# Late columns and block sums as single steps of one written-out order, and a second ScalarE function in the memory units

## The chip, the cores and the metric

The kernel runs on one core of one Trainium2 chip. The engines are TensorE (PE, matmuls), VectorE (DVE), ScalarE (ACT), GpSimd (POOL) and SyncE (SP), which issues the DMAs. Each engine works through its own queue in order. The metric is the device time of one execution in microseconds (us), as the median of several runs.

## The reference

All values are float32. B, H, S, D are 4, 8, 576, 64; there are 2304 tokens; the weights are 512x1536, 512x1536 and 1536x512.

```
scores = where(causal, -1e9, q @ k.T / sqrt(D));  a = softmax(scores)
local = a @ v
q_p = phi(q)                        # phi(x) = max(x, 0) + min(exp(x), 1)
mem_out = (q_p @ M_prev) / (q_p @ z_prev + 1e-6)
x = g * mem_out + (1 - g) * local   # g = sigmoid(beta), per head; heads side by side: 2304 x 512
out = ((x @ w_a) * (x @ w_b)) @ w_out
```

## The kernel before, in words

**Precision.** Each float32 operand of a matmul is split in two parts, a high one (an ACT copy in a shorter format) and a low one (DVE or POOL subtracts the high one). A product is three matmuls: high by high, high by low, low by high.

**Stages.** Attention first, for 16 pairs of heads (`schedule()`): `HEAD` lists the steps of the start by hand, `LOOP` the steps of one pair with lags, for pairs 3 to 8 and, in a second order, 9 to 13, and `TAIL` the steps of the end of attention and of what overlaps it. A step is `name.index`. A step's name stands for instructions on one engine or on two; every engine gets its instructions in the order of the list, and waits for others by semaphores. `BANKS` names the PSUM bank of each step that takes one.

Then come 48 *columns*: column `c` is one block of 384 tokens `t` and one of 12 slices `f` of the weights. `uA.c` and `uB.c` are its two hidden products (12 matmuls each), `ucx` copies B to SBUF (ACT), `umx` multiplies A into it (DVE), `uhh` and `uhl` split the result (ACT, DVE), and `uo.c` adds its output product to three accumulators (9 matmuls). After the last `f` of a `t`, `ua`, `ub`, `uc` bring the accumulators out. The columns cover t = 0 to 3.

The tokens of t = 4 and 5 are handled after them by `step7`, once per `f`: a scheme that multiplies block matrices with fewer products (in the manner of Strassen and Winograd). It needs sums of token blocks (`combine` makes T1, TT2, T3, T4 from the raw blocks B11, B12, B21, B22, which lie in one tile `xf`; `split_x` splits each into `xc`) and sums of weight blocks: `sums_load(f)` fetches the weights of `f` back from HBM into a ring inside `xf`, `sums_of(f)` forms the sums on POOL, `sums_split(f)` splits them (ACT, DVE). Rings 0 and 1 use the same place in `xf`, so the load of 1 waits for the split of 0.

x itself is made by memory *units*: one unit is one of four 128-wide parts `j` of x for one `t`. Its steps are those of `UNIT`: `load` (q by SP, two buffers), `phi`, `phi2`, `norm` to `norm3` (the division), `turn` (a transpose on DVE), `turn_h`, `turn_l` (split), `x_load` and `sums` (the attention part, added on POOL), `retrieve` (3 or 6 matmuls with M_prev), `join`, `join_h`, `join_l`. In `TAIL` a unit's step is `q_<step>.n` with t = 2 + n // 4 and j = n % 4.

**Order around the change.** `TAIL` reaches up to column 29 in its columns and up to unit 5 (and some steps of unit 6). From column `CUT` = 30 on, `column(c, between)` runs a fixed order: A, the planned unit steps of the first half, B, the four conversion steps, `done(c - 1)`; then the unit steps of the second half, then `arrange(c)`, which holds block sums, splits, pool changes and ring loads by column number. `TURN` gives the half columns of the units. In `step7` of f = 0, `sums_split(1)` and the loads of rings 2 and 3 stand ahead of the last token product and of `h1`.

**Before, `phi`** is an exponential on ACT (L1095) and a minimum with 1 on DVE (L1099), then `max(q, 0) + ph` (L1102).

Of the kernel before, what the change touches and what calls it, by code (L numbers as in the profile page):

```python
# [75 lines left out]
Kclamp.5 Khi.4 Kshift.5 Klo.4 uB.3 uhh.2 Kmag.6 uo.1 Khigh.5 Kclamp.6 Kload.7 uhl.2 Kload.10 Klow.5
ucx.3 Khi.5 Kload.9 Kshift.6 umx.3 uA.4 Klo.5 Kload.11 Kmag.7 uB.4 Khigh.6 Kclamp.7 Kload.12 uo.2
uhh.3 uA.5 Klow.6 uhl.3 Khi.6 ucx.4 Kshift.7 Khigh.7 Kmag.8 Kload.14 Klo.6 umx.4 uB.5 Kclamp.8 uhh.4
Klow.7 Kshift.8 Kload.13 uo.3 Khi.7 uA.6 uB.6 uhl.4 Kmag.9 Kclamp.9 ucx.5 Khigh.8 Klo.7 Klow.8
Kload.16 Khi.8 umx.5 uhh.5 uo.4 Kshift.9 Klo.8 uhl.5 Kmag.10 ucx.6 Kload.15 Khigh.9 Klow.9 Khi.9  # L80
Kmag.11 Kclamp.10 Kshift.10 uA.7 umx.6 Khigh.10 Kclamp.11 uB.7 Klo.9 uhh.6 Kload.18 Klow.10
Kshift.11 uhl.6 uo.6 Khi.10 Klo.10 Khigh.11 uA.8 ucx.7 Kmag.12 Klow.11 Khi.11 Kclamp.12 umx.7
Kload.17 Klo.11 Kload.20 uhh.7 uB.8 uo.5 Kshift.12 uhl.7 uA.9 Kmag.13 Khigh.12 Klow.12 uB.9 ucx.8
umx.8 uo.7 uhh.8 Kclamp.13 Khi.12 Kshift.13 Kload.19 Klo.12 Kmag.14 Khigh.13 ucx.9 uhl.8 Kclamp.14
uA.10 Klow.13 Khi.13 Klo.13 Kshift.14 umx.9 Kmag.15 uB.10 uhh.9 uhl.9 Khigh.14 ucx.10 Klow.14
Kclamp.15 uo.9 umx.10 Kshift.15 Khi.14 Klo.14 Kmag.16 Khigh.15 Klow.15 uhh.10 uA.11 Khi.15 uB.11
Kclamp.16 Kmag.17 ucx.11 uo.8 uA.12 Klo.15 uB.12 Kshift.16 uhl.10 Khigh.16 umx.11 Klow.16 Kclamp.17
uhh.11 Kshift.17 uo.10 Khi.16 uA.13 Khigh.17 Kload.22 Klo.16 Kmag.18 Klow.17 ucx.12 uhl.11 Kclamp.18
umx.12 Kshift.18 uhh.12 uB.13 Khi.17 uhl.12 uo.11 Kmag.19 uA.14 Klo.17 uB.14 Khigh.18 Klow.18 Khi.18
Klo.18 Kload.21 ucx.13 Kmag.20 uo.12 Kclamp.19 Kclamp.20 umx.13 uhh.13 Kshift.19 Kshift.20 ucx.14  # L90
Khigh.20 uhl.13 Klow.20 Khi.20 Khigh.19 uA.15 umx.14 Kmag.22 Kclamp.22 Klo.20 uhh.14 Klow.19
Kload.23 uhl.14 Kshift.22 uB.15 Khi.19 ucx.15 uo.13 Klo.19 umx.15 Kmag.21 uhh.15 Khigh.22 Kclamp.21
Klow.22 Khi.22 uA.16 Kshift.21 Khigh.21 uB.16 Klow.21 Khi.21 Kmag.23 uhl.15 Klo.21 uo.14 ucx.16
Kclamp.23 Klo.22 umx.16 Kshift.23 Khigh.23 Klow.23 uo.15 uA.17 Khi.23 Klo.23 uhh.16 uB.17 wo.0
uhl.16 q_load.0 uo.16 q_load.1 q_phi.0 ucx.17 q_phi2.0 q_norm.0 umx.17 Ms.0 q_norm2.0 q_norm3.0
uhh.17 uA.18 q_turn.0 Ml.1 uB.18 Mp.1 uhl.17 q_x_load.0 uo.17 ucx.18 umx.18 q_turn_h.0 ua.17 q_phi.1
q_turn_l.0 q_phi2.1 uhh.18 uA.19 ub.17 q_load.2 uhl.18 q_retrieve.0 q_norm.1 uB.20 q_norm2.1
q_norm3.1 uc.17 q_turn.1 q_sums.0 q_join.0 q_phi.2 uB.19 uA.20 uB.21 Wf.0 Wf.1 ucx.19 q_turn_h.1
umx.19 uhh.19 q_turn_l.1 uhl.19 Wf.2 uo.18 q_x_load.1 q_phi2.2 uo.19 q_norm.2 Ml.2 q_norm2.2
# [1521 lines left out]
```

## Time and profile before

| | |
|---|---|
| median of 3 runs | 669.57 us (669.0 to 669.58) |
| the profiled execution's own time | 671.89 us |
| its span, first to last instruction | 670.1 us |
| PE busy in it | 651.3 us, 97% |
| DVE, ACT, POOL busy | 516.4, 332.4, 277.2 us |
| mean granted clock of TensorE | 0.992 |

A share of busy time is an average over stages with different limits: in the pair loop four engines are busy nearly all of the time, in the columns PE alone. PE's gaps are few and can be read one by one in its timeline, each with the instruction that ended it. [...]

### The profile page before, as it was taken

How to read it: one execution, taken by the hardware profiler on the slowest of the kernel's cores; microseconds unless marked ns; L12 is line 12 of the kernel's file. 1: busy time of each engine (PE TensorE's matmuls, PEld its weight loads, DVE VectorE, ACT ScalarE, POOL GpSimd, SP SyncE). 2: the span in 40 equal slices, each digit the busy share in tenths (PEclk: the TensorE clock that was granted, in tenths of full speed). 3: DMA queues.
4: the chain of work that ended last, by engine and by line, in shares of the span. 5: the costliest groups of instructions: out<-in, count | busy, mean ns of one | idle time of the engine just before them, and what ended most of it. 6: DMA issues, size and time to landing. Idle time of an engine off the chain costs nothing.

```text
span 670.1 us, 11702 instructions
## 1 busy us (share of the span) xinstructions
PE 651.3 (97%) x4074; PEld 598.7 (89%) x4074; DVE 516.4 (77%) x1030; ACT 332.4 (50%) x794; POOL 277.2 (41%) x402
## 2 busy tenths in 40 slices
...
GB/s 180 198 189 133 150 138 187 119 193 188 266 75 134 210 153 110 187 127 59 150 109 206 120 122 30 56 112 66 48 48 31 142 31 65 64 32 63 1 32 63
DMA packets 130250, 76.85 MB, mean 115 GB/s; under 512 B 98704, under 2 KB 117392, under 8 KB 130192
## 3 DMA queue, kind: packets, MB, share of 16 engines
...
q8 instruction: 32, 0.52, 0.3%
q14 instruction: 26, 0.21, 0.1%
HBM read 55.64 MB, written 20.45 MB: 114 GB/s over the span
## 4 chain that ended last, share of the span: by engine, by line
PE 72%; DVE 17%; DMA 3%; ACT 2%; issue 2%; SPq 2%; POOL 1%; DVEq 0%; ACTq 0%; POOLq 0%
PE pp L921 24%; PE pp L1299 12%; PE o L959 12%; PE pt L196 5%; PE pw L710 4%; DVE PT L200 4%; PE pt L544 4%; PE o L1375 4%; DVE nm L583 3%; PE pr L1406 3%; PE m L1375 1%; PE pw L544 1%; DMA qr<-in_q_dram 1%; PE m L1164 1%; DVE wl L200 1%
## 5 line engine op out<-in xcount | busy, mean ns | idle before, releaser
L921 PE MATMUL pp<-xh,wh 128*128 128x384 f32 x376 | 126.9, 337 | 0.9 <-ACT x L934 0.9
L921 PE MATMUL pp<-xh,wl 128*128 128x384 f32 x376 | 126.5, 337 | 0.3 <-DVE wl L200 0.3
L921 PE MATMUL pp<-xl,wh 128*128 128x384 f32 x376 | 126.3, 336 | 0.0
L610 POOL TENSOR_SCALAR P<-P,sum 128x384 f32<-128x384 f32 (+4 forms) x144 | 80.8, 581 | 5.1 <-DVE sum L602 4.5
L1265 POOL TENSOR_TENSOR xf<-xf 128x256 f32<-128x256 f32 x48 | 38.6, 804 | 96.7 <-DMA xf<-ws 63.6
L921 PEld LDWEIGHTS pp<-xh,wh 128*128 128x128 f32 x376 | 70.9, 189 | 3.4 <-ACT x L934 1.9
L921 PEld LDWEIGHTS pp<-xl,wh 128*128 128x128 f32 x376 | 70.9, 189 | 1.6
L921 PEld LDWEIGHTS pp<-xh,wl 128*128 128x128 f32 x376 | 70.8, 188 | 0.6 <-DVE wl L200 0.6
L200 DVE TENSOR_TENSOR PT<-pt,PT 128x512 fp32r<-128x512 f32 (+2 forms) x112 | 62.7, 588 | 10.4 <-ACT PT L665 8.1
L593 ACT ACTIVATE P<-pt,nm 128x128 f32<-128x128 f32 (+3 forms) x128 | 66.9, 530 | 4.9 <-DVE nm L583 3.1
L710 PE MATMUL pw<-PT,vh 128*128 128x320 f32 (+4 forms) x416 | 63.0, 294 | 1.0 <-DVE PT L200 0.6
L710 PEld LDWEIGHTS pw<-PT,vh 128*128 128x128 f32 x416 | 57.6, 189 | 3.6 <-DVE PT L200 1.9
L959 PE MATMUL o<-wh,hh 128*128 128x512 f32 x144 | 57.2, 397 | 3.3 <-ACT hh L941 3.3
L583 DVE TENSOR_REDUCE nm<-pt 128x1 f32<-128x128 f32 (+3 forms) x128 | 55.9, 478 | 3.6 <-PE pt L544 3.3
L959 PE MATMUL o<-wh,hl 128*128 128x512 f32 x144 | 57.7, 400 | 0.0
L959 PE MATMUL o<-wl,hh 128*128 128x512 f32 x144 | 57.0, 396 | 0.0
L865 POOL TENSOR_SCALAR wt<-wt 128x512 f32<-128x512 f32 (+1 forms) x21 | 21.6, 1028 | 83.3 <-ACT wt L859 83.3
L196 PE MATMUL pt<-ident,P 128*128 128x128 f32 (+1 forms) x400 | 52.8, 276 | 2.3 <-POOL P L610 1.0
L665 ACT ACTIVATE PT<-pt 128x512 fp32r<-128x512 f32 (+2 forms) x112 | 52.6, 525 | 2.9 <-PE pw L710 1.7
L941 ACT ACTIVATE hh<-x 128x384 fp32r<-128x384 f32 x48 | 25.0, 522 | 55.4 <-DVE x L937 45.9
L934 ACT ACTIVATE x<-pp 128x384 f32<-128x384 f32 x47 | 22.8, 486 | 53.5 <-PE pp L921 37.5
L196 PEld LDWEIGHTS pt<-ident,P 128*128 128x128 f32 (+1 forms) x400 | 44.1, 140 | 5.8 <-POOL P L610 2.5
...
## 6 DMA issues: line engine op xcount, KB each, us to landing
...
```

The lines of the kernel that those rows point to most:

```text
L196: nc.tensor.transpose(out, x, ident[0:x.shape[0], 0:x.shape[0]])
L200: eng.tensor_tensor(out=lo, in0=x, in1=hi, op=ALU.subtract)
L544: nc.tensor.matmul(o, lhsT=w, rhs=x, start=first, stop=True, skip_group_check=True)
L583: nc.vector.tensor_reduce(out=s["nm"][:, c:c + 1], in_=src, axis=AX.X, op=ALU.min)
L593: nc.scalar.activation(out=s["P", i][:, h, :], in_=src, func=AF.Exp, scale=-1.0, bias=s["nm"][:, c:c + 1], accum_out=s["sums"][:, c, 0:1],)
L610: nc.gpsimd.tensor_scalar(out=pr[:, h, :], in0=pr[:, h, :], scalar1=r[:, c:c + 1], scalar2=1.0, op0=ALU.mult, op1=ALU.mult,)
L665: nc.scalar.activation(out=dst, in_=src, func=AF.Copy)
L710: nc.tensor.matmul(pv[:, a:hi], lhsT=w, rhs=x, start=(n == 0), stop=(n == len(ops) - 1))
L921: nc.tensor.matmul(pp, lhsT=w[:, w0:w0 + P], rhs=x[:, kk, :], start=(c == 0), stop=(c == 3 * KK - 1),)
L959: nc.tensor.matmul(po[t, m], lhsT=hx[:, m * P:(m + 1) * P], rhs=w[:, w0:w0 + DM], start=(f == ORDER[t][0] and n == 0), stop=(f == ORDER[t] ...
L1265: nc.gpsimd.tensor_tensor(out=o, in0=x, in1=y, op=op)
L1299: nc.tensor.matmul(o, lhsT=a[:, kk * P:(kk + 1) * P], rhs=b[:, kk, :], start=first and c == 0, stop=True, skip_group_check=True,)
```

## The change

- `HEAD`, `BANKS` and both orders of `LOOP` are other orders of the same steps, and so is the part of `TAIL` that was there.
- `TAIL` goes on to `uhl.47`: all 48 columns, all units and the block sums are single steps. `co`, `sh`, `sl` are combine, high split and low split of the n-th of B11, T1, TT2, T3, B21, T4, B22; `rl`, `ru`, `rs` are load, sums and split of a ring; `pi`, `cl`, `go` set up tiles and pools. `column`, `arrange`, `TURN` and the plan go. T4 and B22 are still split in `step7`.
- In units of t over 2, `phi` is relu(-q) and then exp(-that) on ACT, and the minimum on DVE goes.
- In `step7` of f = 0, `sums_split(1)` and `sums_load(3)` come behind `hl(0, h1)`, and the last output rows of column 47 behind these.
- The second "ob" pool has one buffer, and units of t over 3 use a new pool.

```diff
 HEAD = """
-id.0 zi.0 wm.14 mk.0 ib.0 Dk.0 zq.1 Dq.0 TK.0 TQ.0 zq.0 Dk.1 b_2.0 thK.0 Dq.1 Eq.0 tlK.0 TK.1 thQ.0
+zq.0 id.0 zi.0 ib.0 wm.14 Dk.0 Dq.0 mk.0 Dk.1 TK.0 Dq.1 TQ.0 thK.0 tlK.0 b_2.0 Eq.0 TK.1 b_3.0 thQ.0
...
 TAIL = """
...
-mag0.15 h2B.14 px.14 G0.15 n2.15 G5.15 clamp0.15 l2B.14 mag1.15 G3A.15 V1B.14 Kload.6 V2B.14 xA.14
-G2A.15 h0.15 shift0.15 G2B.15 h5.15 high0.15 n1.15 h2A.15 low0.15 hi0.15 h3A.15 G4.15 w_0.15 G1.15
...
-py.13 high2.15 V1B.15 V2B.15 xA.15 cx.15 low2.15 hi1.15 st_.14 mx.15 xB.15 lo1.15 hh.15 Kmag.3
-st_.15 Kclamp.3 pp.0 Khi.2 Kshift.3 uA.1 Kload.8 Klo.2 Khigh.3 uB.1 uA.2 ucx.1 hl.15 Klow.3 Kmag.4
...
+n4.15 V2A.14 l2B.14 V1B.14 n2.15 n1.15 mag1.15 shift0.15 high0.15 V2B.14 xA.14 low0.15 G5.15 G2A.15
+st_.12 h2A.15 G2B.15 px.14 clamp1.15 G3A.15 h5.15 G0.15 G4.15 hi0.15 h0.15 G1.15 G3B.15 l2A.15
...
+py.13 high2.15 V2B.15 low1.15 mx.15 st_.14 xA.15 xB.15 hh.15 hl.15 st_.15 low2.15 pp.0 hi1.15 lo1.15
+uA.1 Khi.2 Kload.7 Kmag.3 Kload.6 uB.1 Klo.2 Kclamp.3 ucx.1 Kshift.3 Khigh.3 uA.2 Kload.8 Kmag.4
...
+q_join.7 Ws.22 Ws.23 umx.33 uA.34 uo.31 q_join_h.7 q_join_l.7 uA.35 go.0 uhh.33 q_load.8 q_phi.8
+q_phi2.8 uB.34 q_norm.8 uhl.33 ucx.34 q_x_load.8 q_norm2.8 q_load.9 uo.32 umx.34 uhh.34 q_norm3.8
+q_turn.8 uB.35 q_phi.9 q_turn_h.8 uo.33 ucx.35 uB.36 q_x_load.9 uhl.34 uA.36 uB.37 q_sums.8 q_phi2.9
+umx.35 q_load.12 q_x_load.12 uA.37 q_load.13 uhh.35 q_sums.9 q_norm.9 q_turn_l.8 q_retrieve.8 uhl.35
+q_norm2.9 q_norm3.9 q_turn.9 q_sums.12 ucx.36 q_phi.12 umx.36 q_join.8 uo.34 q_turn_h.9 uhh.36 uo.35
+ucx.37 q_phi.13 pi.0 q_phi2.12 q_norm.12 q_turn_l.9 q_norm2.12 q_norm3.12 uc.35 uhl.36 q_x_load.13
+q_retrieve.9 q_turn.12 umx.37 q_join.9 q_turn_h.12 q_phi2.13 ua.35 uA.38 uhh.37 q_load.14 uA.39
+q_x_load.14 uB.38 uo.36 q_norm.13 sh.0 ucx.38 uhl.37 q_turn_l.12 uo.37 ub.35 q_norm2.13 uB.39 umx.38
+uhh.38 q_phi.14 ucx.39 q_norm3.13 q_retrieve.12 q_turn.13 uA.40 uhl.38 q_turn_h.13 umx.39 uB.40
+uhh.39 q_sums.13 q_phi2.14 q_load.15 q_x_load.15 uo.38 q_turn_l.13 uB.41 q_sums.14 q_load.10
+q_x_load.10 q_join.12 q_norm.14 ucx.40 q_retrieve.13 uhl.39 uo.39 q_norm2.14 umx.40 uhh.40 sl.0
+uA.41 q_norm3.14 q_turn.14 q_join.13 uB.42 uhl.40 q_turn_h.14 co.1 q_phi.15 q_sums.15 ucx.41
+q_turn_l.14 q_phi2.15 q_retrieve.14 uB.43 q_norm.15 q_norm2.15 umx.41 uo.40 q_norm3.15 uA.42 uhh.41
+q_turn.15 ucx.42 q_join.14 q_turn_h.15 uhl.41 q_phi.10 q_phi2.10 q_turn_l.15 umx.42 sh.1 uhh.42
+q_norm.10 ucx.43 uhl.42 q_retrieve.15 q_norm2.10 q_norm3.10 q_load.11 q_x_load.11 uA.43 umx.43
+q_sums.10 uo.41 q_phi.11 q_turn.10 q_join.15 q_phi2.11 uB.44 uo.42 uA.44 uhh.43 q_norm.11
+q_turn_h.10 uhl.43 q_norm2.11 q_norm3.11 sl.1 q_turn_l.10 ucx.44 uB.45 q_sums.11 q_retrieve.10
+q_turn.11 umx.44 co.3 q_join.10 q_turn_h.11 uo.43 uhh.44 q_turn_l.11 q_retrieve.11 uA.45 uB.46 sh.3
+co.2 uB.47 q_join.11 cl.0 uA.46 sh.2 sl.2 uhl.44 sh.4 ucx.45 umx.45 sl.3 sl.4 co.5 uo.44 rl.0 ru.0
+uA.47 uhh.45 ucx.46 uhl.45 umx.46 uhh.46 uhl.46 ucx.47 uo.45 umx.47 uo.46 rs.0 uhh.47 rl.1 ru.1
+uhl.47
 """
...
         def phi():
             ph = r["ph"] = pool.tile([P, J, U, Q4], F32, tag="ph", name="ph")
-            nc.scalar.activation(out=ph, in_=r["q"], func=AF.Exp)
+            if late:
+                nc.scalar.activation(out=ph, in_=r["q"], func=AF.Relu, scale=-1.0)
+                nc.scalar.activation(out=ph, in_=ph, func=AF.Exp, scale=-1.0)
+            else:
+                nc.scalar.activation(out=ph, in_=r["q"], func=AF.Exp)
 
         def phi2():
             ph = r["ph"]
-            nc.vector.tensor_scalar(
-                out=ph, in0=ph, scalar1=1.0, scalar2=None, op0=ALU.min
-            )
+            if not late:
+                nc.vector.tensor_scalar(
+                    out=ph, in0=ph, scalar1=1.0, scalar2=None, op0=ALU.min
+                )
...
-        sums_split(f + 1)
-        if f == 0:
+        if f:
+            sums_split(f + 1)
+            sums_load(f + 3)
+        else:
             sums_load(2)
-        sums_load(f + 3)
         prev[3]()
...
         hh(0, h1)
-        prev[4]()
-        hl(0, h1)
+        if f == 0:
+            hl(0, h1)
+            sums_split(1)
+            sums_load(3)
+            prev[4]()
+        else:
+            prev[4]()
+            hl(0, h1)
...
         attention(late, early, tiles, {"TK": first_weights, "S_4": turn_over}, more, beyond)
-        for c in range(CUT, len(columns)):
-            column(c, lambda: memory(c, True))
-            memory(c, False)
-            arrange(c)
```

## Rows read from the trace of the kernel before

**Rows 1.** The page's first part: the span, and PE's busy time.

```profile
span 670.1 us, 11702 instructions
PE 651.3 (97%) x4074; PEld 598.7 (89%) x4074; DVE 516.4 (77%) x1030; ACT 332.4 (50%) x794; POOL 277.2 (41%) x402
```

**Rows 2.** Windows: length, busy us (and instructions) of each engine, clock, DMA.

```profile
0.00:20.00 20.00, 17.20 (x128) 13.55 (x129) 14.56 (x36) 13.35 (x38) 11.47 (x24) 1.00 0.83 180
20.00:40.00 20.00, 18.74 (x162) 16.33 (x162) 19.21 (x44) 19.76 (x59) 17.87 (x30) 1.00 0.84 189
...
480.00:500.00 20.00, 17.39 (x82) 14.72 (x82) 16.37 (x39) 4.81 (x10) 2.53 (x2) 0.92 0.21 50
...
520.00:540.00 20.00, 16.57 (x76) 15.58 (x76) 11.27 (x18) 6.63 (x13) 9.42 (x12) 0.83 0.37 119
```

**Rows 3.** PE's timeline in the late columns: start, duration, instruction, idle before.

```profile
464.91 0.50 PE L959 MATMUL o<-wh,hh 128*128 128x512 f32 x1 [1.01 <-ACT hh L941]
...
480.64 0.45 PE L1164 MATMUL m<-yh,md 128*128 128x384 f32 x1 [0.19 <-ACT yh L1148]
...
481.69 0.34 PE L921 MATMUL pp<-xh,wh 128*128 128x384 f32 x1
...
495.40 0.50 PE L959 MATMUL o<-wh,hh 128*128 128x512 f32 x1 [2.25 <-ACT hh L941]
```

**Rows 4.** PE's timeline after the first step 7; 18 matmuls start from 532.22 on.

```profile
532.22 0.69 PE L1299 MATMUL pp<-xh,wh 128*128 128x384 f32 x1 [3.42 <-DVE h L1339]
...
538.04 0.34 PE L1299 MATMUL pp<-xeh,wh 128*128 128x384 f32 x1
```

**Rows 5.** The chain that ended last, 494 to 540: start, us, what.

```profile
496.16 2.72 PE o L959 x7
498.88 4.90 PE pp L921 x24
503.78 2.10 PE o L959 x9
...
506.54 4.20 PE pp L921 x24
...
520.82 3.19 DMA xf<-ws
```

**Rows 6.** Windows over the late columns and over four pairs of the loop.

```profile
432.00:518.00 86.00, 82.38 (x428) 75.04 (x427) 62.20 (x143) 21.99 (x44) 11.09 (x11) 0.98 0.24 60
30.20:76.80 46.60, 45.95 (x402) 41.18 (x402) 45.94 (x106) 45.38 (x129) 44.73 (x69) 1.00 0.67 168
```

**Rows 7.** Groups by line, 330 to 530: busy us, mean ns, idle before.

```profile
L1099 DVE TENSOR_SCALAR ph<-ph 128x384 f32<-128x384 f32 x14 | 6.6, 470 | 1.5 <-ACT ph L1095 1.5
...
L1095 ACT ACTIVATE ph<-q 128x384 f32<-128x384 f32 x13 | 6.7, 513 | 10.6 <-DVE q L1144 9.0 <-DMA z<-in_z_prev_dram 1.5
```

**Rows 8.** The program's only table load: ns, first and last start.

```profile
L520 ACT ACT_TABLE_LOAD  x1: 1283/1283/1283, 0.7 to 0.7; - x1
```

**Rows 9.** POOL's timeline at the sums of ring 0.

```profile
513.63 3.18 POOL L1265 TENSOR_TENSOR xf<-xf 128x256 f32<-128x256 f32 x4 [17.94 <-DMA xf<-ws]
```

**Rows 10.** DVE's timeline in the first step 7.

```profile
519.46 1.29 DVE L200 TENSOR_TENSOR wl<-xf,wh 128x768 fp32r<-128x768 f32 x2 [0.18 <-ACT wh L1278]
...
528.24 1.41 DVE L200 TENSOR_TENSOR sl<-xf,sh 128x768 fp32r<-128x768 f32 x1 [2.46 <-ACT sh L1278]
...
531.61 0.56 DVE L1339 TENSOR_TENSOR h<-pp,h 128x384 f32<-128x384 f32 x1
```

**Rows 11.** Timelines of POOL, PE and ACT where attention turns into columns.

```profile
192.56 0.94 POOL L353 TENSOR_SCALAR xh<-xx 128x384 fp32r<-128x384 f32 x1
...
196.61 1.86 PE L196 MATMUL pt<-ident,P 128*128 128x128 f32 x15 [0.98 <-POOL P L610]
...
210.55 0.49 ACT L934 ACTIVATE x<-pp 128x384 f32<-128x384 f32 x1 [0.76 <-POOL hl L200]
211.09 0.45 PE L921 MATMUL pp<-xh,wh 128*128 128x384 f32 x1 [0.86 <-ACT x L934]
```

More of the change, by code (lines that the diff above doesn't have):

```diff
@@ L76 @@
[L76 to L99, printed above, removed]
@@ L112 @@
[L112 to L114 removed]
+h3A.11 TK.14 b_3.13 l3A.11 S_3.13 pd.12 e4.12 r_.12 px.10 n3.12 pe.11 thK.14 pb.12 m3B.13 pf.11
+pc.12 TQ.14 V1A.11 V2A.11 tlK.14 n1.12 m3A.13 e3B.13 thQ.14 fw.0 b_.13 b_2.13 S_2.13 n4.12 xA.11
+m2A.13 Lp.13 m2B.13 e3A.13 e2A.13 S_.13 V1B.11 n0.12 e2B.13 mA.13 py.10 G5.12 V2B.11 eA.13 mB.13
@@ new lines @@
+Kshift.9 Khigh.9 Khi.8 Klo.8 uhl.5 Klow.9 Kmag.10 Khi.9 ucx.6 Klo.9 umx.6 Kload.12 Kmag.11 Kclamp.10
+Kload.15 Kshift.10 uA.7 Khigh.10 Klow.10 uB.7 uhh.6 uo.5 uA.8 uhl.6 Khi.10 Kclamp.11 Kshift.11
+Khigh.11 Klo.10 Klow.11 Kload.14 uB.8 ucx.7 Kmag.12 umx.7 uhh.7 uhl.7 uo.6 Khi.11 Klo.11 Kmag.13
+ucx.8 Kclamp.12 Kshift.12 Khigh.12 Klow.12 umx.8 uA.9 uB.9 uo.7 Kclamp.13 Kshift.13 Khigh.13
+Kload.17 uhh.8 Khi.12 uhl.8 Kmag.14 Klo.12 Klow.13 ucx.9 uA.10 umx.9 Khi.13 Kmag.15 uB.10 uhh.9
+Klo.13 uhl.9 Kload.16 uo.8 ucx.10 uA.11 Kclamp.14 Kshift.14 Khigh.14 Klow.14 Kclamp.15 Khi.14 umx.10
@@ new lines @@
+Kshift.15 uhh.10 Khigh.15 Kmag.16 Kclamp.16 Klo.14 Klow.15 uhl.10 uB.11 Khi.15 uo.9 Kshift.16 ucx.11
+Kmag.17 Klo.15 Kclamp.17 Khigh.16 umx.11 Kload.18 Klow.16 Khi.16 uhh.11 Kshift.17 Kmag.18 Khigh.17
+Kload.19 Klo.16 uA.12 uB.12 ucx.12 uo.10 uhl.11 Klow.17 umx.12 Khi.17 uhh.12 Kmag.19 uA.13 Kclamp.18
+uB.13 Kshift.18 Kclamp.19 Khigh.18 Klo.17 Klow.18 Khi.18 uo.11 uA.14 Kload.21 uhl.12 Kload.20 ucx.13
+uB.14 Kmag.20 Kshift.19 Klo.18 umx.13 uhh.13 Khigh.19 Klow.19 uhl.13 Kclamp.20 Kshift.20 Kload.22
@@ new lines @@
+Khigh.20 Klow.20 ucx.14 uo.12 Khi.19 umx.14 Klo.19 uA.15 Khi.20 Kmag.21 uhh.14 Kclamp.21 Kmag.22
+Klo.20 uhl.14 Kshift.21 uB.15 uo.13 ucx.15 Khigh.21 Kclamp.22 Klow.21 uA.16 Khi.21 Kshift.22
+Khigh.22 umx.15 uhh.15 uB.16 Klo.21 Klow.22 Kload.23 Kmag.23 uhl.15 Kclamp.23 Khi.22 ucx.16 Klo.22
+uo.14 uA.17 umx.16 uB.17 Kshift.23 Khigh.23 Klow.23 Khi.23 Klo.23 uhh.16 uo.15 wo.0 uhl.16 q_load.0
+q_phi.0 ucx.17 umx.17 q_x_load.0 uhh.17 q_phi2.0 q_norm.0 uA.18 uB.18 ucx.18 q_load.1 q_norm2.0
+uo.16 q_norm3.0 q_turn.0 uhl.17 q_sums.0 q_x_load.1 uo.17 umx.18 q_turn_h.0 q_phi.1 Ml.1 q_turn_l.0
@@ new lines @@
+uA.19 uhh.18 ua.17 q_phi2.1 q_norm.1 ub.17 uB.19 uc.17 Ms.0 q_norm2.1 Wf.0 Mp.1 q_retrieve.0
+q_norm3.1 q_load.2 Ws.0 Wf.1 uhl.18 Wf.2 q_join.0 q_turn.1 Wf.3 uB.20 Ws.3 q_turn_h.1 q_phi.2 ucx.19
+umx.19 q_phi2.2 q_join_h.0 q_norm.2 Ml.2 q_sums.1 uhh.19 Ws.2 q_turn_l.1 uhl.19 q_norm2.2 ucx.20
+q_join_l.0 uA.20 umx.20 uB.21 Wf.4 q_norm3.2 Wf.5 uhh.20 uo.18 Ws.1 uo.19 q_load.3 q_retrieve.1
+q_phi.3 Wf.6 q_join.1 uA.21 q_turn.2 uhl.20 q_phi2.3 q_turn_h.2 q_turn_l.2 q_x_load.2 Ws.5 Wf.7
+q_join_h.1 ucx.21 q_norm.3 uA.22 uB.23 umx.21 uB.22 q_sums.2 q_norm2.3 uhh.21 ucx.22 q_join_l.1
@@ new lines @@
+q_norm3.3 uo.20 Wf.8 uhl.21 umx.22 Ws.4 uhh.22 q_turn.3 Wf.9 Ws.7 uhl.22 q_retrieve.2 q_join.2
+q_turn_h.3 q_join_h.2 q_load.4 Ws.8 Wf.10 ucx.23 Ws.6 uo.21 Ws.9 uA.23 q_x_load.3 q_turn_l.3 umx.23
+uo.22 q_join_l.2 q_phi.4 uhh.23 q_phi2.4 q_sums.3 q_retrieve.3 q_load.5 uhl.23 uo.23 Wf.11 q_join.3
+q_join_h.3 q_join_l.3 uA.24 uB.24 q_norm.4 Ws.10 ua.23 ub.23 uc.23 ucx.24 q_norm2.4 umx.24 uhh.24
+p2.0 uB.25 uhl.24 ucx.25 uA.25 umx.25 uB.26 Wf.12 uA.26 q_norm3.4 uo.24 q_turn.4 Ws.11 uhh.25 Wf.13
+uA.27 uhl.25 Ws.13 q_turn_h.4 Wf.14 Wf.15 ucx.26 umx.26 q_phi.5 q_phi2.5 uB.27 q_x_load.5 q_norm.5
@@ new lines @@
+q_load.6 q_norm2.5 uB.28 q_turn_l.4 Mp.2 q_norm3.5 Ws.12 Ws.15 q_turn.5 uo.25 uhh.26 uhl.26 ucx.27
+umx.27 uB.29 q_phi.6 q_retrieve.4 q_phi2.6 uA.28 uhh.27 ucx.28 uhl.27 q_turn_h.5 uB.30 uo.26
+q_norm.6 q_norm2.6 uA.29 umx.28 uhh.28 uA.30 Ml.3 Wf.16 q_x_load.4 q_turn_l.5 uhl.28 Wf.17 ucx.29
+q_sums.4 q_norm3.6 q_join.4 q_load.7 umx.29 Ws.14 Wf.18 q_turn.6 Wf.19 q_turn_h.6 q_sums.5
+q_join_h.4 Ws.17 q_retrieve.5 q_turn_l.6 uo.27 Mp.3 uhh.29 uB.31 q_phi.7 Ws.16 q_phi2.7 uo.28 uhl.29
+Ws.18 Wf.20 q_join.5 q_norm.7 uA.31 q_norm2.7 uB.32 ucx.30 q_join_h.5 q_join_l.4 umx.30 q_norm3.7
```

194 lines of the change are left out of this document (74 added, 120 removed).

## The prediction, made before the change was run

> **What bounds the kernel now.** I read the page first: TensorE (PE) is busy for 651.3 of a span of 670.1 us [rows 1]. The order of a list cannot make a matmul shorter, so what an order can win is the rest, about 19 us, and whatever the clock loses. The table of windows says where that is: the first 40 us (17.20 and 18.74 busy of 20), then 480 to 500 (17.39, granted clock 0.92) and 520 to 540 (16.57, clock 0.83) [rows 2]. So I went to PE's timeline at those places and looked at what is named behind each "idle before".
>
> Three waits lie in the late columns. At 464.91 PE idles 1.01 for `hh`. At 480.64 it idles 0.19 for `yh`, and the three matmuls of a retrieve then take 1.05 (480.64 to 481.69). At 495.40 it idles 2.25 for `hh` again [rows 3]. The fourth is in the first step 7: 3.42 before 532.22, for the `h` of L1339 [rows 4].
>
> The last two cost more than their idle. After 495.40 nine output matmuls need 0.76+2.72 where nine take 2.10 a little later, and the next 24 need 4.90 where 24 take 4.20 [rows 3, 5]. After 532.22 eighteen matmuls need 5.82 (to 538.04 [rows 4]) where at 4.20 per 24 they would need 3.15. [...] Both times PE had stood idle for more than 2 us just before; after the idle of 1.01 nothing like it is seen.
>
> **The change, part by part.** *Columns 30 to 47.* Today each column runs A, B, its four conversion steps and at once `done(c-1)`, so three blocks of matmuls lie between a column's B and its output matmuls (`done(c-1)`, the next A, the next B), 6.3 us at 2.10 each [rows 5]. Whole groups of unit steps ("phi phi2 norm norm2") go into the queue of VectorE (DVE) at one point; the multiply of a column stands behind them, then comes `hh` of ScalarE (ACT), then the output matmuls. That is the wait at 464.91 and 495.40. In the new list seven blocks lie between `uB.34` and `uo.34`, six between `uB.40` and `uo.40`: 12.6 us or more, and unit steps stand singly between column steps. DVE has room: it is busy 62.20 of 86.00 us between 432 and 518, ACT 21.99 [rows 6]. What the three waits cost today: 1.01 and about 0.2 to get going again at 464.91; 0.19 and 1.05-0.52 at 480.64; 2.25+1.38+0.70 at 495.40. Sum 1.2+0.7+4.3 = 6.2. I take all of it as won.
>
> The same edit can set new waits. q loads have two buffers, so on SyncE's (SP's) queue a `q_load` waits for the `turn_l` of a unit before it, and `x_load` and all later loads and stores wait behind it; `q_phi` is ACT's, waits for its load, and holds up the `ucx` behind it, which frees the bank for a later B. The trace of before has no such order, so I bound it: 0, if the covers hold; one wait like the worst of today, 4.3, if one does not. I take 1.2, a wait like the smaller one, since most covers are several blocks long but `q_retrieve.11` stands only one block behind `q_retrieve.10`, with five DVE operations between.
>
> *exp(-relu(-q)) for units of t over 2*: twelve units lose a `min` on DVE (0.47 each, L1099) and get a second ACTIVATE of the size of L1095 (0.51) [rows 7]: 5.6 us off DVE, 6.2 onto ACT. ACT's part is covered by its 64 idle us of 86 [rows 6]; without that cover it would cost up to 6.2. The trace shows no Relu. A reload of ACT's table, 1.28 each [rows 8], could come twice per unit, 24 in all or 31 us, half of ACT's idle time; the other bound is 0. I take 0, as one load serves all that ACT does today: its Copy, its Abs of the weights and its Exp. [...]
>
> *Block sums and step 7.* Ring 0's sums are ready at 513.63+3.18 = 516.81 [rows 9], but its split comes behind the last column on ACT and DVE, whose subtractions run from 519.46 [rows 10]; only then can ring 1 load (520.82, 3.19 us) into the same place [rows 5]. Its sums take as long again, and `sums_split(1)` begins on DVE at 528.24 with an operation of 1.41. `h` at L1339 is queued behind it, done at 531.61+0.56 [rows 10], and PE's next part waits for the bank that `h` reads. The new list puts `rs.0` behind `umx.47` but ahead of `uhl.47`, with `uA.47` two blocks before the end, so ring 1 can start some 2 us earlier; and `sums_split(1)` goes behind `hh` and `hl` of step 0. So `h` no longer waits for it. Late next is the first use of the split itself, in the second part of the next step. From the end of the `a22` part PE then has a third of an output block, 0.70, a part `ga` and a part `al` of 1.05 each, and two matmuls: 3.15 in all. Against it stand two operations for `h`, then `hh` and `hl`, at 0.56 each, and the split at 1.41: 3.65. That is 0.5 late, and I allow 0.9 for the handing over. Won: 3.42+2.67-0.9 = 5.2. The load of ring 3 goes behind `hl` too; its sums are asked for one step later, so that costs nothing.
>
> *The turn from attention to columns.* At 211.09 PE idles 0.86 for ACT's `x`, which began at 210.55 after waiting 0.76 for `hl` on GpSimd (POOL) [rows 11]. There `hl.15` stands behind `Kclamp.3`; in the new list it follows `hh.15` directly. `x` itself (0.49) must still follow the B block, so I count 0.4, and 0.2 for the low weights, as `Klo.2` is now ahead of `Kshift.3`: 0.6. Earlier, at 196.61, PE waits 0.98 for POOL's normalization; `px.14`, 0.94 on POOL at 192.56 [rows 11], moves from ahead of `n2.15` to behind `n1.15`. I count 0.9; bounds 0 and 1.0. The same POOL work stands ahead of `py.14` in both lists, so the low half of x that column 1 reads comes no later.
>
> *HEAD, BANKS, LOOP.* The first 40 us idle 4.1 in all [rows 2], much of it the first loads, whose order on SP is all but the same. In the pair loop PE is busy 45.95, DVE 45.94, ACT 45.38 and POOL 44.73 of 46.60 [rows 6]: at most 0.65 in four pairs can be won, and there is no slack to hide a loss. Value 0; bounds 2 won (half of that idle), 5 lost (one DVE operation of 0.47 [rows 7] a pair more, in eleven pairs).
>
> Sum: -6.2 +1.2 -5.2 -0.6 -0.9 = -11.7. The profiled execution took 671.89, so its like would be 660.2; it stands 2.32 above the median of the three runs, 669.57, and I take the difference over: 657.9.
>
> **Rivals.** *A new wait in the columns, with its clock loss.* For it: DVE was busy 72% of the time between 432 and 518 [rows 6] and still late, and SP serves loads in order. Against: covers of several blocks. One of 4.3 instead of my 1.2 gives 661.0, two give 665.3. Chance 0.18.
>
> *The stretches at the lower clock belong to the profiled execution alone.* It is 2.32 longer than the median. Then 1.38+0.70+2.67 = 4.8 of the gain was never in the timed runs: 662.7. Against: a program on one core with the same waits should see them every time. Chance 0.08.
>
> *The sums stay late.* If ring 0's load goes out no earlier, because `co.5` on DVE stands behind the last units, the split of ring 1 stops PE two parts later than `h` does today: the 5.2 are lost, 663.1. Chance 0.07.
>
> *Relu is the longer way.* A unit's first link grows by an ACTIVATE of 0.51 [rows 7]; if ACT is what every unit waits for, twelve times 0.51 is 6.2: 664.1. Against: the `min` of 0.47 that it replaces is all but equal, and ACT is the idler engine [rows 6]. [...] Chance 0.04.
>
> *Slower: the pair loop.* Four engines at 96 to 99% leave nothing; a new order that makes one of them wait once per pair pays eleven times. From 11.7/11 = 1.1 us a pair on the change is lost; at 1.4 it is 673.3. Against: the new loop keeps the same order of stages. Chance 0.05.
>
> **How the numbers follow.** The forecast has the remaining 0.58, with a range of its own from 654.5 to 660.5 (HEAD wins 2 and no new wait comes; or half of the 5 is lost in the loop). The range for 8 in 10 reaches from 653.5 to 664.5: it takes in the first four rivals but for two new waits, and leaves out the slower one. A measurement of this kernel tells about 0.2%, 1.3 us, from no change. Faster by more: 0.58+0.18+0.08+0.07+0.04, less 0.02 for several of them at once, 0.93; same 0.02; slower 0.05.
>
> **What would show it.** Right: no idle above 1 us on PE between 430 and the end of the columns; the first step 7 followed by the second with less than 1 us idle, put down to the split (`sh` or `sl`), not to `h`; granted clock 1.00 in every window after the start; DVE without L1099 in the twelve units; still one table load; the first `x` of the columns no longer waiting for POOL. Wrong: a wait of 2 us or more for `yl`, `hl` or a q load with a window below 1.00 behind it; or a pair period above the old one. The forecast fails as a whole if the waits of attention grow, since nothing later can pay for them.

## The result, and the profile after

The changed kernel takes 660.63 us (median of 4 runs, 660.08 to 662.75) beside 669.29 of the kernel before (4 runs, 668.28 to 669.58): a ratio of 0.9879, with an interval from 0.9855 to 0.9904. The forecast was 657.9, the range 653.5 to 664.5. The changed kernel is faster, inside the range, and 2.7 us above the forecast. (One execution of the kernel before, at a mean clock of 0.754, is left out of everything below.)

The profiled execution of the changed kernel took 660.38 us, 11.5 less than that of the kernel before (671.89); the sum had said 11.7 less. So the sum held between the two profiled executions, and what did not hold is the step from there to the median. The page's first part after, to be read against [rows 1]:

```profile
span 658.6 us, 11688 instructions
PE 644.8 (98%) x4074; PEld 594.7 (90%) x4074; DVE 510.8 (78%) x1018; ACT 337.7 (51%) x806; POOL 278.9 (42%) x402
```

PE runs the same 4074 matmuls in 6.5 us less busy time. Of this, 5.0 lie in the columns and in step 7 (2.5 each): a matmul at the lower clock counts as busy for longer (in the execution of [rows 4], 0.52 us from 533 to 537, where the granted clock is 0.50, and 0.34 from 538.04 on, where it is 1.00), and these stretches are gone. The rest lies in attention, where the clock reads 1.00 in both, and was not followed up. The windows after show the granted clock as a share of full speed (columns as in [rows 2]; the 86 us window answers to the first of [rows 6]):

```profile
20.00:40.00 20.00, 19.72 (x177) 17.37 (x175) 19.73 (x44) 19.64 (x56) 18.79 (x32) 1.00 0.86 190
432.00:518.00 86.00, 84.67 (x452) 78.65 (x451) 63.63 (x145) 29.84 (x57) 14.55 (x15) 1.00 0.26 65
480.00:500.00 20.00, 20.00 (x111) 18.76 (x111) 17.75 (x41) 7.37 (x14) 1.16 (x1) 1.00 0.11 26
500.00:520.00 20.00, 20.00 (x105) 18.48 (x104) 10.02 (x15) 5.75 (x10) 7.54 (x8) 1.00 0.24 79
520.00:540.00 20.00, 18.70 (x99) 17.17 (x99) 14.83 (x25) 6.76 (x15) 10.56 (x12) 1.00 0.29 93
```

Between 480 and 500 PE now starts 111 matmuls where it started 82, and the granted clock, once 0.92 and 0.83, is 1.00. Between 430 and 540 PE has three waits left, one in the columns and two in the first step 7 (PE's timeline: start, duration, instruction, idle before):

```profile
445.65 0.44 PE L945 MATMUL pp<-xh,wh 128*128 128x384 f32 x1 [1.19 <-DVE x L961]
...
523.98 0.44 PE L1333 MATMUL pp<-wh,sl 128*128 128x384 f32 x1 [0.84 <-DVE sl L224]
...
525.40 0.41 PE L1333 MATMUL pp<-xh,wh 128*128 128x384 f32 x1 [0.46 <-DVE u L1404]
```

The three idles of [rows 3] and the 3.42 of [rows 4] are gone. To see where the 11.5 came from, two starts on PE cut both executions in three stages: the first output matmul of column 0, and the first matmul of step 7. They are these two lines of the kernel before, and then the same two after:

```profile
216.00 0.39 PE L959 MATMUL o<-wh,hh 128*128 128x512 f32 x1
...
518.96 0.34 PE L1299 MATMUL pp<-xh,wh 128*128 128x384 f32 x1
```

```profile
213.81 0.39 PE L983 MATMUL o<-wh,hh 128*128 128x512 f32 x1
...
512.09 0.34 PE L1333 MATMUL pp<-xh,wh 128*128 128x384 f32 x1
```

With the spans (670.1 and 658.6) this gives, in us; the lines below the first two are of runs told further on, worked out in the same way:

| profiled execution | up to column 0's output | columns | step 7 to the end |
|---|---|---|---|
| kernel before | 216.0 | 303.0 | 151.1 |
| changed kernel | 213.8 | 298.3 | 146.5 |
| changed kernel, a second one | 215.4 | 297.7 | 146.8 |
| kernel before, a second one | 216.3 | 302.8 | 150.2 |
| before, new step 7 order only | 216.1 | 303.2 | 146.5 |
| before, new attention only | 214.9 | 303.1 | 150.1 |
| changed, old step 7 order | 214.4 | 297.8 | 145.6 |
| changed, late sums and old step 7 | 213.7 | 297.8 | 149.1 |
| changed, old attention | 214.9 | 297.8 | 146.6 |
| columns only | 214.9 | 297.7 | 147.5 |

Columns 4.7, step 7 4.6, the first stage 2.2: 11.5. The sum had 5.0, 5.2 and 1.5 for them. That it came within 0.2 of 11.5 is in part luck: the misses cancel, and the first stage alone differs by 1.6 between two executions of the changed kernel. All the same, that stage took 216.0 to 216.3 us in the three executions with the old turn from attention to columns, and 213.7 to 215.4 in the seven with the new one.

### The profile page after: what moved, and what is told of

The parts are those of the page before. It is cut to its first block, busy times and chain, and to the rows that moved or that the text cites. A ratio compares the mean times of both kernels' runs of the same rounds, so it can differ in the third digit from the quotient of the medians.

```text
span 658.6 us, 11688 instructions
## 1 busy us (share of the span) xinstructions
PE 644.8 (98%) x4074; PEld 594.7 (90%) x4074; DVE 510.8 (78%) x1018; ACT 337.7 (51%) x806; POOL 278.9 (42%) x402
## 4 chain that ended last, share of the span: by engine, by line
PE 76%; DVE 13%; ACT 4%; SPq 2%; issue 2%; POOL 1%; DMA 1%; ACTq 0%; POOLq 0%
PE pp L945 24%; PE pp L1333 13%; PE o L983 12%; PE pt L220 6%; PE pw L734 6%; PE pt L568 4%; PE o L1416 4%; DVE PT L224 3%; PE pr L1447 3%; DVE nm L607 2%; PE m L1416 1%; PE pw L568 1%; DVE wl L224 1%; POOL P L634 1%; PE m L1193 1%
## 5 line engine op out<-in xcount | busy, mean ns | idle before, releaser
L634 POOL TENSOR_SCALAR P<-P,sum 128x256 f32<-128x256 f32 (+4 forms) x144 | 82.0, 596 | 2.2 <-DVE f L226 1.0
L1299 POOL TENSOR_TENSOR xf<-xf 128x256 f32<-128x256 f32 x48 | 41.1, 856 | 91.5 <-DMA xf<-ws 55.7
L607 DVE TENSOR_REDUCE nm<-pt 128x1 f32<-128x384 f32 (+3 forms) x128 | 55.6, 477 | 3.4 <-PE pt L568 3.3
```

What stands on the lines that cost most here:

```text
L607: nc.vector.tensor_reduce(out=s["nm"][:, c:c + 1], in_=src, axis=AX.X, op=ALU.min)
L634: nc.gpsimd.tensor_scalar(out=pr[:, h, :], in0=pr[:, h, :], scalar1=r[:, c:c + 1], scalar2=1.0, op0=ALU.mult, op1=ALU.mult,)
L1299: nc.gpsimd.tensor_tensor(out=o, in0=x, in1=y, op=op)
```

## The experiments

Ratios are to the kernel before on the same chip.

**The kernel before again (b0_control).** No edit.

> The kernel before, unchanged, to see how its executions differ from one another. The profiled execution of before took 671.89 us, 2.3 to 2.6 above the median of its timed runs, while that of the changed kernel (660.38) lies at its median; so the gain is 11.5 by the profiles and 8.7 by the medians. Theory: the stretches at the lower clock are not the same in every execution of before; then the runs show different clocks (some at 0.995 or above, with spans near 667.5, one or the other at 0.992 with a span near 670). Rival: every execution has both stretches, with a clock of 0.992 and spans of 670, and the 2.3 lies outside the span.

Ratio 1.0009 (0.999 to 1.0027); the profiled execution had a mean granted clock of 0.995, not 0.992. Each execution's mean clock is recorded. Over three chips, 51 executions of the kernel before go by their clock like this:

| mean granted clock | executions | mean us | lowest and highest |
|---|---|---|---|
| 0.992 | 15 | 671.5 | 670.5, 672.5 |
| 0.995 | 15 | 670.4 | 669.4, 671.8 |
| 0.997 | 19 | 669.3 | 668.2, 671.1 |
| 1.000 | 2 | 667.5 | 667.1, 667.9 |

The execution that the prediction read was of the first row. The clocks of the four executions behind 669.29 are not on record; their times lie about the mean of the third row. The changed kernel had 0.999 or 1.000 in all of its 8 executions. The second profile of the kernel before shows which stretch varies (windows, columns as in [rows 2]):

```profile
480.00:500.00 20.00, 17.34 (x82) 14.69 (x82) 16.86 (x40) 4.41 (x9) 2.39 (x2) 0.91 0.21 50
500.00:520.00 20.00, 20.00 (x110) 18.75 (x109) 8.84 (x15) 7.10 (x13) 2.95 (x4) 1.00 0.08 26
520.00:540.00 20.00, 16.55 (x81) 15.44 (x80) 11.92 (x19) 6.72 (x13) 9.69 (x12) 0.91 0.37 119
```

The window of the first step 7 has 0.91 here and 0.83 in [rows 2], after nearly the same idle (3.45 and 3.42 us); the window from 480 has about the same clock in both. The 18 matmuls behind step 7's wait take 4.82 us here, and 5.82 in the execution of [rows 4]:

```profile
532.33 0.45 PE L1299 MATMUL pp<-xh,wh 128*128 128x384 f32 x1 [3.45 <-DVE h L1339]
...
537.15 0.34 PE L1299 MATMUL pp<-xeh,wh 128*128 128x384 f32 x1
```

**The Relu away (e_no_relu).** The `min` on VectorE is back, one ACTIVATE goes:

```diff
-        late = t > 2
+        late = False
```

> The changed kernel with the minimum on DVE in all units (one ACTIVATE and two DVE operations, as before). Forecast's theory: the second ACTIVATE is covered and the 12 x 0.47 us on DVE matter only where DVE is late, so the time is within 1.5 us of the changed kernel, somewhat longer (0 to +1.5; the wait of 1.19 for the multiply of a column grows by 0.5 to 1). Rival 1, DVE's relief carries the gain: +3 to +5.6, with new waits for DVE in the columns. Rival 2, Relu is the longer way: up to 6 shorter.

660.7 us, ratio 0.9866 (0.9845 to 0.9887), beside 0.9879 and 0.9868 for the changed kernel: no difference that can be told. In the window 432 to 506 it moves work from ACT (25.43 busy us to 22.15) to DVE (57.38 to 60.16), and PE's busy time is 72.67 and 72.83. The edit is a trade between two engines that both have room.

**The new step 7 order alone, on the kernel before (e_step7_order_only), and the changed kernel with the old one (e_old_step7_order).** The first is the diff's step 7 part put into the kernel before; the second takes it out of the changed kernel:

```diff
-        if f:
-            sums_split(f + 1)
-            sums_load(f + 3)
-        else:
+        sums_split(f + 1)
+        if f == 0:
             sums_load(2)
+        sums_load(f + 3)
...
-        if f == 0:
-            hl(0, h1)
-            sums_split(1)
-            sums_load(3)
-            prev[4]()
-        else:
-            prev[4]()
-            hl(0, h1)
+        prev[4]()
+        hl(0, h1)
```

> The kernel before with the new order in step 7 of f = 0 alone. Theory A, both edits are needed: some 2 to 3.5 us are won, and a wait of 1.5 to 3 remains for the split. Theory B, the order carries all: 4 to 5 us are won, the wait that remains is 1 to 1.5 and the clock stays up. Theory C, the earlier ring carries all: 0 to 1 won.

> The changed kernel with the old order in step 7 of f = 0 (the split of ring 1 ahead of the last token product and of h). Theory A, both edits are needed: the sums of ring 1 are ready 1.8 us earlier than before (6.6 after the end of the columns instead of 8.4), so h waits about 2.0 instead of 3.4, the waits of 0.84 and 0.46 behind it go: +0.5 to +1.5 us, and the clock may or may not fall. Theory B, the order in step 7 carries all: h waits 3 or more and the clock falls, +4.5 to +5.5. Theory C, the earlier ring carries all: 0 or shorter.

Alone it gives a ratio of 0.9955 (0.9937 to 0.9973), about 3.0 us; in its profiled execution PE waits 0.65 for `sl` and 0.47 for `u` instead of 3.42 for `h`:

```profile
531.17 0.44 PE L1299 MATMUL pp<-wh,sl 128*128 128x384 f32 x1 [0.65 <-DVE sl L200]
...
532.60 0.41 PE L1299 MATMUL pp<-xh,wh 128*128 128x384 f32 x1 [0.47 <-DVE u L1370]
```

That is the gain of theory A with the wait of theory B. The table suggests why they part: from step 7 on, this execution is 4.6 us shorter than the execution of the kernel before at 0.992, and 3.7 shorter than the one at 0.995. But taking it out of the changed kernel costs nothing: 659.71 us, 0.9857 (0.9835 to 0.9879), and PE then waits for `h` alone, 0.58 us:

```profile
522.44 0.44 PE L1333 MATMUL pp<-xh,wh 128*128 128x384 f32 x1 [0.58 <-DVE h L1373]
```

So with the new columns the earlier sums, the other half of that edit, do away with the long wait without the new order.

**Both halves undone (f_late_sums_old_step7), beside the changed kernel again (f_after_again).** To the diff above comes

```diff
-uA.47 uhh.45 ucx.46 uhl.45 umx.46 uhh.46 uhl.46 ucx.47 uo.45 umx.47 uo.46 rs.0 uhh.47 rl.1 ru.1
-uhl.47
+uA.47 uhh.45 ucx.46 uhl.45 umx.46 uhh.46 uhl.46 ucx.47 uo.45 umx.47 uo.46 uhh.47 uhl.47 rs.0 rl.1
+ru.1
```

> The changed kernel with both halves of the step 7 edit undone: the split of ring 0 and the load and sums of ring 1 stand behind the last column step again, and the first step 7 has its old order. Theory A (either half alone removes the long wait, both undone bring it back, and the low clock behind it comes in some executions only): an idle of about 3.4 us on TensorE before the part that waits for h of the first step 7, against 0.8 and 0.5 now; the median 2 to 3.5 us above the changed kernel, 662.6 to 664.2; executions with a clock of 0.995 or less are about 2 us longer than those at 0.999. Theory B (the low clock follows that wait in every execution): 4.7 above, 665.3. Theory C (what delayed h were the block sums of other units on VectorE, which the new list has moved away, so the wait stays gone): 660.6, idle under 1.5 us.

> The changed kernel once more, nothing edited, so that the other kernels of this chip have their base beside them. Theory A (what the median keeps of the profiled gain depends on how much of the lower-clock stretches each execution of the kernel before has; the new kernel has none): 660.0 to 661.0 us, a mean granted clock of 0.999 or 1.0 in every execution, and a ratio of 0.985 to 0.989. Theory B (the clock comes and goes by itself, whatever the waits): some executions of this kernel too below 0.998 and 1 to 3 us longer.

The changed kernel: 661.18 us, 0.9868 (0.9853 to 0.9883), clocks 0.999 or 1.000. With both halves undone: 662.37 us, 0.9888 (0.9871 to 0.9905), clocks 0.997, 0.997, 0.997 and 1.000. The wait is back, but only 2.51 long, and the cost is 1.2 us, less than the 2 to 3.5 expected, and not clear of noise, as the two intervals overlap. (By the table, this profiled execution is 2.3 and 2.6 us longer from step 7 on than the two of the changed kernel.) The wait is shorter because the last column's work ends sooner: by the trace, the last column's subtraction on DVE starts at 509.94, 1.6 us ahead of the first step 7 matmul (511.51), where before it was 0.2 (518.73 and 518.96). So the split of ring 0 and the load of ring 1 come sooner even when they stand last (on DVE the split starts 0.8 ahead of step 7, where before it was 0.5 behind), and part of what the sum gave to the step 7 edit belongs to the columns.

**Columns only (g_columns_only).** The last kernel with, in addition, the old orders of `HEAD`, `BANKS`, `LOOP` and of `TAIL` up to `pp.0` (with `hl.15` right behind `hh.15`):

```diff
 TAIL = """
-h3A.11 TK.14 b_3.13 l3A.11 S_3.13 pd.12 e4.12 r_.12 px.10 n3.12 pe.11 thK.14 pb.12 m3B.13 pf.11
+px.10 pe.11 h3A.11 b_3.13 S_3.13 TQ.14 l3A.11 pf.11 e4.12 st_.10 m3B.13 Lv.15 Lp.13 r_.12 pb.12
```

> The changed kernel with the old orders of attention, the late sums and the old order of the first step 7 all at once; what is left of the change is the order of the column steps and unit steps up to column 47, the turn from attention to columns, and the Relu. Theory A (the columns are where most of the gain is, the three idles there and the clock behind the last): 0.5 to 1 above the kernel with late sums and old step 7 alone, 662.4 to 663.4 us, ratio 0.988 to 0.991; no idle over 1.3 between 430 and the end of the columns, one of 2.5 in the first step 7. Theory B (the parts are worth little alone and the gain comes from all together): over 665. Theory C (attention's order is worth nothing): 662.4 or less.

663.42 us, 0.9904 (0.9881 to 0.9927): 0.0096 of the 0.012 to 0.013 that the whole change gives, about three quarters, and the turn and the Relu are in it. This run and the one before it have the same wait in the first step 7, and happen to show what the clock does with it. PE's timeline of the kernel with late sums and old step 7:

```profile
523.67 0.45 PE L1333 MATMUL pp<-xh,wh 128*128 128x384 f32 x1 [2.51 <-DVE h L1373]
...
524.85 0.50 PE L1333 MATMUL pp<-wh,sh 128*128 128x384 f32 x1
525.14 0.53 PE L1333 MATMUL pp<-wl,sh 128*128 128x384 f32 x1
525.46 0.53 PE L1333 MATMUL pp<-wh,sl 128*128 128x384 f32 x1
...
528.50 0.33 PE L1333 MATMUL pp<-xeh,wh 128*128 128x384 f32 x1
```

and of the columns-only kernel:

```profile
524.75 0.44 PE L1333 MATMUL pp<-xh,wh 128*128 128x384 f32 x1 [2.50 <-DVE h L1373]
...
525.90 0.34 PE L1333 MATMUL pp<-wh,sh 128*128 128x384 f32 x1
526.08 0.34 PE L1333 MATMUL pp<-wl,sh 128*128 128x384 f32 x1
526.26 0.34 PE L1333 MATMUL pp<-wh,sl 128*128 128x384 f32 x1
...
528.00 0.33 PE L1333 MATMUL pp<-xeh,wh 128*128 128x384 f32 x1
```

The same 18 matmuls after the same idle: 4.83 us in the one, 3.25 in the other. Once 525 is past, starts lie 0.32 apart in the first, as they do in the execution of [rows 4] from 533 to 537, where the granted clock is 0.50, and 0.17 to 0.18 in the second. The windows from 525 to 535 of the two, in the same order, give the clock, 0.84 and 1.00:

```profile
525.00:535.00 10.00, 10.00 (x47) 9.51 (x46) 5.84 (x11) 2.67 (x6) 3.03 (x4) 0.84 0.30 104
```

```profile
525.00:535.00 10.00, 10.00 (x55) 9.51 (x55) 6.67 (x13) 3.42 (x8) 3.22 (x4) 1.00 0.46 159
```

**Attention's order, taken out (f_old_attention) and alone (g_attention_only).** The first is the diff above alone; the second puts the new orders up to `pp.0` into the kernel before:

```diff
 TAIL = """
-px.10 pe.11 h3A.11 b_3.13 S_3.13 TQ.14 l3A.11 pf.11 e4.12 st_.10 m3B.13 Lv.15 Lp.13 r_.12 pb.12
+h3A.11 TK.14 b_3.13 l3A.11 S_3.13 pd.12 e4.12 r_.12 px.10 n3.12 pe.11 thK.14 pb.12 m3B.13 pf.11
...
-py.13 high2.15 V1B.15 V2B.15 xA.15 cx.15 low2.15 hi1.15 st_.14 mx.15 xB.15 lo1.15 hh.15 Kmag.3
-st_.15 Kclamp.3 pp.0 Khi.2 Kshift.3 uA.1 Kload.8 Klo.2 Khigh.3 uB.1 uA.2 ucx.1 hl.15 Klow.3 Kmag.4
+py.13 high2.15 V2B.15 low1.15 mx.15 st_.14 xA.15 xB.15 hh.15 hl.15 st_.15 low2.15 hi1.15 lo1.15
+Kmag.3 Kclamp.3 Kload.6 pp.0 Khi.2 Kshift.3 uA.1 Kload.8 Klo.2 Khigh.3 uB.1 uA.2 ucx.1 Klow.3 Kmag.4
```

> The changed kernel with the orders of the kernel before for attention: the start, the banks, both loop orders and the first part of the last list up to the step that hands x over; hl.15 keeps its new place, so the turn to the columns should keep its gain. Theory A (the sums of excess time between TensorE's starts: 0.5 lost at the end of attention and 0.9 in the first 140 us): 1.4 us longer than the changed kernel, 662.0. Theory B (the forecast: only the one wait of 0.98 at the end of attention, the loop costs the same): 0.9 longer, 661.5. Theory C (attention's order is worth nothing, and the differences in it are those of one execution): 660.6. Theory D (the new loop order loses and hides a gain): faster than the changed kernel, below 660.

> The kernel before with the new orders of the start, the banks, the loop and the first part of the last list, hl.15 directly behind hh.15 with it; columns, Relu and step 7 as before. Theory A (by the sums of excess time: 0.8 at the turn, 0.4 at the end of attention, nothing firm ahead of it): 1.2 below the kernel before, ratio 0.998. Theory B (the forecast: 0.6 and 0.9): 1.5 below, ratio 0.9978. Theory C (the first 140 us win 0.9 as well): 2.1 below, ratio 0.9968. Theory D (nothing): 1.000. The interval will hardly part A from B; whether the wait of 0.98 for GpSimd at the end of attention is there is read from the trace, and B wants it gone.

Taken out: 661.9 us, 0.9882 (0.9865 to 0.9898), 0.7 above the changed kernel and inside its interval. Alone: 670.07, 0.9996 (0.9976 to 1.0015): no gain that can be measured. The trace of the changed kernel shows that the 0.9 for the wait at the end of attention was wrong. Its waits of PE between 140 and 215 (what waited for what: us in total, times, longest):

```profile
PE pt L220 <- POOL P L634: 1.0, 2, 0.5
PE pw L734 <- ACT xo L743: 0.8, 1, 0.8
PE pp L945 <- ACT x L958: 0.6, 1, 0.6
```

The 0.98 for POOL of [rows 11] is now 0.5 twice, and 0.8 for ACT has come beside it. With the new orders alone it is 0.67 and 0.58 for POOL and 0.83 for ACT.

**A better one (f_best, g_best_2).** DVE's timeline ahead of the idle at 445.65, of the changed kernel:

```profile
442.92 0.23 DVE L1158 TENSOR_SCALAR n<-n,over_gate 128x12 f32<-128x12 f32 x1
443.19 0.23 DVE L1162 RECIPROCAL n<-n 128x12 f32<-128x12 f32 x1
443.45 0.56 DVE L1167 TENSOR_TENSOR ph<-ph,n 128x384 f32<-128x384 f32 x1
443.93 0.55 DVE L224 TENSOR_TENSOR hl<-x,hh 128x384 fp32r<-128x384 f32 x1
444.40 0.57 DVE L1173 STREAM_TRANSPOSE q<-ph 128x384 f32<-128x384 f32 x1
445.04 0.56 DVE L961 TENSOR_TENSOR x<-pp,x 128x384 f32<-128x384 f32 x1
```

The copy of column 37, `ucx.37` on ACT, waits for the `hl` at 443.93:

```profile
444.51 0.49 ACT L958 ACTIVATE x<-pp 128x384 f32<-128x384 f32 x1 [4.18 <-DVE hl L224]
```

`uhl.36` (443.93) stands behind the division of unit 12; `ucx.37` needs the buffer that it reads, `umx.37` (445.04) needs `ucx.37` and stands behind the transpose as well. f_best puts `uhl.36` first and takes the old step 7 order; g_best_2 also moves `umx.37`:

```diff
-ucx.37 q_phi.13 pi.0 q_phi2.12 q_norm.12 q_turn_l.9 q_norm2.12 q_norm3.12 uc.35 uhl.36 q_x_load.13
+ucx.37 q_phi.13 pi.0 q_phi2.12 q_norm.12 q_turn_l.9 uhl.36 q_norm2.12 q_norm3.12 uc.35 q_x_load.13
```

```diff
-q_turn_l.9 uhl.36 q_norm2.12 q_norm3.12 uc.35 q_x_load.13
-q_retrieve.9 q_turn.12 umx.37 q_join.9
+q_turn_l.9 uhl.36 q_norm2.12 umx.37 q_norm3.12 uc.35 q_x_load.13
+q_retrieve.9 q_turn.12 q_join.9
```

> The changed kernel with two edits: the low split of column 36 (uhl.36) moves ahead of the two division steps of unit 12 in the list, and the first step 7 has its old order again, with the earlier sums kept. Theory A (umx.37 was late by what stood ahead of uhl.36 on VectorE, and the moved split of step 7 costs 0.9 more than it saves once the sums are early): the idle of 1.19 us at 445.65 goes, step 7 waits 0.6 for h instead of 0.84 and 0.46, together about 2.2 less: 658.4. Theory B (the division steps are now late themselves, and a retrieve or a q load waits in place of it): the idle moves to a matmul of a memory unit, 659.7 or no gain, 660.6.

> The changed kernel with the low split of column 36 ahead of the division steps of unit 12, the multiply of column 37 ahead of the last of them and of the turn, and the old order in the first step 7. Theory A (the 0.70 idle that is left at 444.81 is the multiply behind four operations of unit 12 in VectorE's queue): that idle goes, 0.8 less than with the low split alone: 658.4. Theory B (the unit's chain is late now): an idle of the same size before the retrieve of unit 12 or 13, 659.2.

f_best: 659.24 us, 0.9839 (0.9824 to 0.9854), 1.9 less than the changed kernel on that chip. The old step 7 order alone had 0.9857 (0.9835 to 0.9879), so what the move of `uhl.36` adds by itself is not clear of noise. The idle is 0.70 instead of 1.19, not gone:

```profile
444.81 0.44 PE L945 MATMUL pp<-xh,wh 128*128 128x384 f32 x1 [0.70 <-DVE x L961]
```

g_best_2: 659.07, 0.9839 (0.9817 to 0.986), no better: that idle is 0.46, and one of 0.47 has come at 449.90 for a copy of the accumulators on DVE.

## Why the forecast came out 2.7 us low

- *The step to the median* is the one that failed: "it stands 2.32 above the median of the three runs, 669.57, and I take the difference over". The difference is not a constant of the run; it is time at the lower clock that this execution had and most others had less of (the executions at 0.992 and at 0.997 stand 2.2 apart), above all in the 2.67 after step 7's wait, and the change takes that away. It was counted twice: as a gain, and as an offset that stays. Without it the forecast is 660.2, and the profiled execution took 660.38, the median 660.63. What shows it: the clocks of 51 executions against 8, and the pair of traces with one idle and two clocks. The same pair refutes what the prediction held against the rival "the stretches belong to the profiled execution alone": "a program on one core with the same waits should see them every time". That rival was half right. The stretch after 495 is in both profiles of the kernel before (0.92 and 0.91); after step 7's wait the one at 0.995 loses about 1.7 us where the other loses 2.67. Which of the two stretches an execution at 0.997 has is not shown: e_step7_order_only, with the long wait in the columns alone, and f_late_sums_old_step7, with the one in step 7 alone, both have executions at 0.997.
- *Columns.* Forecast 5.0 with the new wait, measured 4.7 in the profiled pair. The new wait of 1.2 came, at 1.19, but not where the sum looked (a q load, or `q_retrieve.11`): it is `uhl.36` behind the division of unit 12. That the size agrees is luck: 1.2 was taken from a wait of the kernel before. It cost no clock (1.00 from 432 to 518), so the rival with 4.3 fell.
- *Step 7.* Forecast 5.2, of which 2.67 clock; measured 4.6 in the pair, 2.1 of it idle and 2.5 busy time of PE at the lower clock; 3.0 by medians for the order alone. The mechanism held: `h` no longer waits, PE waits for the split (0.84) and then for `u` (0.46), 1.3 where 0.9 was allowed. The rival of late sums fell: ring 1's sums are ready at 518.71, 6.6 after the end of the columns, where they took 8.4 before, even though ring 1's four additions take 4.61, where ring 0's took 3.18 before [rows 9] (why is not shown):

```profile
514.10 4.61 POOL L1299 TENSOR_TENSOR xf<-xf 128x256 f32<-128x256 f32 x4 [5.81 <-DMA xf<-ws]
```

- *The turn.* Forecast 0.6. In the changed kernel PE's idle for `x` fell from 0.86 to 0.64, and ACT's `x` waits for PE's own block and no longer for POOL. The kernel with the old attention shows the turn by itself: the 0.27 for the low weights is gone as well, and from the end of the idle for POOL to column 0's first output it takes 18.66 us (196.26 to 214.92) instead of 19.39 (196.61 to 216.00), so 0.7. First a line of the kernel before, then three of that one:

```profile
211.98 0.45 PE L921 MATMUL pp<-xh,wl 128*128 128x384 f32 x1 [0.27 <-DVE wl L200]
```

```profile
196.26 1.86 PE L220 MATMUL pt<-ident,P 128*128 128x128 f32 x15 [0.98 <-POOL P L634]
...
210.53 0.44 PE L945 MATMUL pp<-xh,wh 128*128 128x384 f32 x1 [0.64 <-ACT x L958]
...
214.92 0.39 PE L983 MATMUL o<-wh,hh 128*128 128x512 f32 x1
```

- *The end of attention.* Forecast 0.9; the wait only changed its owner. By medians the turn and this are too small to tell.
- *HEAD, BANKS, LOOP.* Forecast 0, and nothing measurable in either direction; the rival of a slower pair loop fell.
- *Relu.* Forecast 0, measured 0. There is still one table load, 1283 ns at the start, with 12 Relu and 12 Exp right after them behind it. On which engine the clamp runs made no difference (660.7 us with the `min` on VectorE, 660.63 and 661.18 with the Relu).

What stays open is what decides, from one execution to the next, whether and for how long the lower clock follows an idle of 2.2 to 3.5 us: nothing that these runs vary settles it.
